# Ten short weight-merge chains placed elsewhere in a hand-written TensorE order (two attention blocks, one core)

## The chip, the cores and the metric

The kernel runs on one core of one Trainium2 chip. Its engines work side by side, each with its own instruction queue, in order: TensorE (PE, matmuls into PSUM), VectorE (DVE), ScalarE (ACT), GpSimd (POOL) and SyncE (SP), whose queue issues most DMAs. The metric is the device time of one launch in microseconds (us); lower is better. The time before is 253.73 us, the median of 3 runs (253.66 to 253.92).

## The reference, cut to what matters

Two independent attention blocks, A and B, each on an input of 2048 tokens x 640, with 32 heads of 20. A is softmax attention in a sliding window of 256 keys; B is linear attention. The two results are set side by side.

```python
def _A_ref(x, wqkv, wo):
    H = 32; Dh = D // H; W = 256
    qkv = (x @ wqkv).reshape(B, S, 3, H, Dh)              # -> q, k, v by head
    scores = einsum("bhqd,bhkd->bhqk", q, k) * Dh ** -0.5  # masked to 0 <= i - j < W
    p = softmax(scores)
    o = einsum("bhqk,bhkd->bhqd", p, v)
    return o.reshape(B, S, D) @ wo

def _B_ref(x, wqkv, wo):
    phi = lambda t: where(t > 0, t + 1, exp(t)) + 1e-6
    pq, pk = phi(q), phi(k)
    kv = einsum("bhsd,bhse->bhde", pk, v)
    z = einsum("bhsd->bhd", pk)
    num = einsum("bhqd,bhde->bhqe", pq, kv)
    den = einsum("bhqd,bhd->bhq", pq, z) + 1e-6
    return (num / den).reshape(B, S, D) @ wo

concatenate([_A_ref(...), _B_ref(...)], axis=-1)
```

All inputs are bfloat16.

## The kernel before

Tokens are worked in four blocks of 512 (`SB`), s = 0 to 3. The 640 input columns are five tiles of 128 (`KT`).

The frame of the program is A's attention. A list of units (`tiles_of`) fills a PSUM tile `S_ps` of four banks with scores (L789), ACT takes one exponential over all of it (L797), GpSimd clears the masked corners (`affine_select`, L812), and two units later `values` multiplies by v (L836). There is one `S_ps`, so the next unit's scores wait for the exponential. DVE turns the values (L849), divides by the row sums (L860, L866) into `N`, and DMA transposes (L877) make the layout `oT` for A's output product.

Between the units runs everything else, in the order of a hand-written `plan`: a list of entries with a due time (no unit, merely a place in the order). `at(t0, t1, gen, n)` spreads n steps of a generator evenly over t0 to t1. `fill_of` sorts the entries, and after each unit `take` draws so many matmul columns from them that all of the work is used up by the end. One step is in general one PSUM bank: a chain of five matmuls and its copy to SBUF. A chain may be cut by the next unit. The bank comes from a pool of four (`dps`, tile name `dense`), shared with the values; a chain can only start when the bank's last user has been read.

Who empties a bank is settled while the program is written. `evac` gives a plain copy to ACT (L259) or DVE (L261), by two counters of the work that each was given. `phi` (B's keys and queries) needs both: an exponential on ACT (L284), then two operations on DVE (L288, L291), the second of which reads the bank again. DMA issues that hang on these are put off by some banks with `soon` and then go to SP's queue in that order.

B's second half is what the change touches. `b_kv` builds the key-value product by head into `kv_T`; two selects on GpSimd (L623) keep each head's own block. `b_merge` then multiplies `kv_T` by B's output weights: ten banks (five tiles of 128 rows, two halves of 320 columns), each of two matmuls (L675) and a copy into the place of B's key weights in `wB`. `b_out` (B's output, through L274) reads these merged weights.

B's queries: `b_q(s)` makes five chains (L274, xB and wB), each with its `phi` and a DMA transpose of the result to tokens (L706, `tok`). `b_den` makes the denominators (L718, L729, L730). `quotients` multiplies the tokens by the reciprocals on DVE, four operations (L754), and turns each back with a DMA transpose (L758). `again_x` (L953) loads a block of x again from DRAM scratch. `a_out(s)` is A's output product of a block, five banks; `a_v(3)` A's last value projection (L409).

In plan times, the neighbourhood of the merges (46.0 to 52.8 before) is: `b_q(1)` 45 to 50, `a_v(3)` 43 to 49, `a_out(0)` (A's first output) 44.5 to 48.5, `b_den(0)` at 46.3, `a_out(1)` (A's second output) 50.2 to 54.8, `b_q(2)` 52 to 57, `b_den(1)` at 53, `b_out(0)` 54.8 to 59.2.

Of the kernel before, what the change touches and what calls it, by code (L numbers as in the profile page):

```python
# [92 lines left out]
def kernel(  # L93
# [12 lines left out]
    KT = D // P  # L106
# [146 lines left out]
    def evac(dst, src, n=SB, to=None):  # L253

        if to is None:
            to = "A" if load["A"] < load["D"] + AHEAD else "D"
        load[to] += n + COPY
        if to == "A":
            nc.scalar.activation(out=dst, in_=src, func=ACT.Copy)  # L259
        else:  # L260
            nc.vector.tensor_copy(out=dst, in_=src)  # L261

    def bank(wide=False):
        flush(begun[0] - 2)
        begun[0] += 1
        settle(False)
        if wide:
            return dps.tile([P, 2 * SB], BF16, name="dense")
        return dps.tile([P, SB], F32, name="dense")
# [396 lines left out]
    def b_merge():  # L666

        for c in range(KT):
            for lo in (0, D // 2):
                cols = slice(lo, lo + D // 2)  # L670
                ps = bank()
                for i in range(2):

                    at = PAD + (P - GD) * c - i * GD
                    nc.tensor.matmul(  # L675
                        ps[:, 0 : D // 2],
                        lhsT=kv_T[0:GD, c + i, at : at + P],
                        rhs=wo_sb["B"][0 : GH * DH, c + i, cols],
                        start=(i == 0),
                        stop=(i == 1),  # L680
                    )
                evac(w_sb["B"][:, c, D + lo : D + lo + D // 2], ps[:, 0 : D // 2], D // 2)
                yield End(D)
# [60 lines left out]
    def quotients(s):  # L744


        def one(tb):
            settle()
            add_load(d=1400)
            if tb == 0:  # L750
                oT_B[s] = xp.tile([P, KT, SB], BF16, name="xA")
            v = tok_of[s][:, tb, 0:D]
            vh = v.rearrange("p (h e) -> p h e", e=DH)
            nc.vector.tensor_tensor(  # L754
                out=vh, in0=vh, in1=rden_of[s][:, tb, :, :].to_broadcast([P, H, DH]), op=ALU.mult
            )
            out = oT_B[s][:, :, tb * P : (tb + 1) * P]
            soon(lambda: nc.sync.dma_start_transpose(out=out, in_=v), 1)  # L758

        quotients_due.extend((s, tb, one) for tb in range(TPS))  # L760
# [272 lines left out]
    plan = []  # L1033

    def at(t0, t1, gen, n):
        for i in range(n):
            plan.append((t0 + (i + 0.5) / n * (t1 - t0), gen, i == n - 1))

    def do(t0, t1, fns):
        fns = list(fns)  # L1040
        for i, fn in enumerate(fns):
            plan.append((t0 + (i + 0.5) / len(fns) * (t1 - t0), None, fn))
# [30 lines left out]
    for s, tq, td, tx in ((0, (39.5, 45), 46.3, 47.7), (1, (45, 50), 53, 54.3),  # L1073
# [1 line left out]
        at(*tq, b_q(s), KT)  # L1075
        at(td, td + 0.1, b_den(s), 1)
        do(tx, tx, [lambda s=s: quotients(s)])
    at(46.0, 52.8, b_merge(), 2 * KT)
    for n, s, t0, t1 in (("A", 0, 44.5, 48.5), ("A", 1, 50.2, 54.8), ("B", 0, 54.8, 59.2),
                         ("B", 1, 60.2, 64), ("A", 2, 64.4, 68.2), ("B", 2, 69, 73),  # L1080
                         ("B", 3, 73, 76)):
# [40 lines left out]
    for i, (s, parts, selects, done) in enumerate(units):  # L1122
# [7 lines left out]
        if ready and ready[0][0] + LAG <= i:  # L1130
# [3 lines left out]
            _, at = ready.popleft()  # L1134
# [10 lines left out]
    while ready:  # L1145
        take(5500)
        _, at = ready.popleft()
# [36 lines left out]
```

## Time and profile before

| | |
|---|---|
| time, median of 3 runs | 253.73 us (253.66 to 253.92) |
| profiled execution, time | 253.77 us |
| profiled execution, span | 252.1 us |
| granted TensorE clock | 0.998 |
| PE busy | 247.5 us (98%), 3733 matmuls |
| ACT busy | 196.6 us (78%) |
| POOL busy | 186.3 us (74%) |
| DVE busy | 167.4 us (66%) |
| merges (L675) in the trace | 20 matmuls, 162.1 to 184.1 us |

The span is what the profiler saw from the first to the last instruction; the time of the launch has 1.67 us more. The page's busy time of an engine says how long it had an instruction in work. In a row of the timeline come the start, the length, the engine, the line, the operation, the output and inputs with their shape and the number of instructions put together; a bracket gives the idle time ahead of the row and what ended it. Rows of PE overlap a little, as matmuls are pipelined: the distance from start to start is the better measure there. A row of the waits names who waited, for whom, the total, how often, and the longest.

### The profile page before, as it was taken

What the parts mean: (1) busy time and instruction counts of PE and PEld (TensorE: products, weight loads), DVE (VectorE), ACT (ScalarE), POOL (GpSimd) and SP (SyncE); (2) the same over time, 40 slices, a digit from 0 to 9 for tenths busy, and PEclk for the clock granted to TensorE, in tenths of its full rate; (3) what the DMA queues carried; (4) which work ended last, traced back from release to release, by engine and by line L of the source; (5) the groups of instructions that cost most, each with busy time, mean ns of one, the idle gap of its engine ahead of it and who ended that gap; (6) DMA issues with size and microseconds to landing.
All of it is one profiled execution on the core that took longest, in us unless ns stands there. A gap on an engine that the chain in (4) does not pass through costs nothing.

```text
span 252.1 us, 8786 instructions
## 1 busy us (share of the span) xinstructions
PE 247.5 (98%) x3733; PEld 142.4 (56%) x3733; DVE 167.4 (66%) x310; ACT 196.6 (78%) x194; POOL 186.3 (74%) x310
## 2 busy tenths in 40 slices
PE   8999999999999999999999999999999999999994
PEld 7644446557755446457445555556455565655573
DVE  0345777768644566776664766666879688869662
ACT  3376779898867788997658887889998998999541
POOL 1126798879877798686778969888887978999800
PEclk9999999999999999999999999999999999999999
DMA  6996598899650252997759595621957398869614
GB/s 204 321 264 160 107 194 130 157 213 245 91 104 3 70 167 34 235 248 186 80 124 165 107 202 99 168 26 38 194 109 157 83 194 173 114 161 146 196 56 155
DMA packets 68412, 37.04 MB, mean 147 GB/s; under 512 B 51605, under 2 KB 67349, under 8 KB 68373
## 3 DMA queue, kind: packets, MB, share of 16 engines
q1 hardware_dynamic: 67685, 35.67, 68.5%
q10 hardware_dynamic: 688, 0.82, 1.0%
q8 instruction: 29, 0.48, 0.8%
q14 instruction: 10, 0.08, 0.1%
HBM read 14.42 MB, written 9.83 MB: 96 GB/s over the span
## 4 chain that ended last, share of the span: by engine, by line
PE 93%; DVE 2%; ACT 2%; issue 1%; ACTq 0%
PE dense L274 52%; PE S_ps L789 11%; PE dense L564 9%; PE dense L836 9%; PE dense L409 7%; PE dense L196 1%; PE first L409 1%; PE dense L718 1%; PE first L178 1%; PE dense L675 1%; PE dense L647 1%; DVE phi L291 1%; DVE e L288 0%; ACT e L284 0%; PE dense L903 0%
## 5 line engine op out<-in xcount | busy, mean ns | idle before, releaser
L812 POOL TENSOR_SCALAR_AFFINE_SELECT p<-p 128x256 bf16<-128x256 bf16 (+2 forms) x280 | 176.5, 660 | 41.9 <-ACT p L797 40.4
L797 ACT ACTIVATE p<-S_ps 128x2048 bf16<-128x2048 f32 x76 | 142.8, 1879 | 33.8 <-PE S_ps L789 31.5
L274 PE MATMUL dense<-xA,wqk 128*128 128x512 bf16 x200 | 50.9, 380 | 0.1
L789 PEld LDWEIGHTS <-kpad 20*128 20x128 bf16 (+1 forms) x1216 | 21.7, 98 | 29.6 <-issue 26.0
L789 PE MATMUL S_ps<-qpad,kpad 20*65 20x64 bf16 (+3 forms) x1216 | 33.7, 228 | 0.0
L288 DVE TENSOR_SCALAR e<-e 128x512 bf16<-128x512 bf16 x40 | 18.6, 465 | 21.4 <-ACT e L284 21.2
L849 DVE STREAM_TRANSPOSE T<-dense 128x512 f32<-128x512 f32 x32 | 22.8, 712 | 15.0 <-PE dense L836 14.8
L274 PEld LDWEIGHTS <-wqk 128*128 128x128 bf16 x200 | 17.9, 98 | 19.5 <-POOL wqk L353 0.4
L291 DVE SCALAR_TENSOR_TENSOR phi<-dense,e 128x512 bf16<-128x512 f32 x40 | 27.7, 692 | 1.6
L274 PE MATMUL dense<-xB,wB 128*128 128x512 bf16 x100 | 26.3, 380 | 0.0
L836 PE MATMUL dense<-p,vA 128*32 128x64 bf16 (+2 forms) x1216 | 25.9, 231 | 0.0
L274 PE MATMUL dense<-wB,xB 128*128 128x512 bf16 (+1 forms) x160 | 25.9, 300 | 0.0
L564 PE MATMUL dense<-tok,phi 128*128 128x129 bf16 (+1 forms) x160 | 25.5, 300 | 0.0
L274 PE MATMUL dense<-wo,oT 128*128 128x512 bf16 (+4 forms) x165 | 25.1, 296 | 0.0
L284 ACT ACTIVATE e<-dense 128x512 bf16<-128x512 f32 x40 | 23.6, 597 | 1.2 <-PE dense L274 1.0
L274 PE MATMUL dense<-wB,xA 128*128 128x512 bf16 (+1 forms) x160 | 24.3, 299 | 0.0
L409 PE MATMUL dense<-wA,xA 128*128 128x320 bf16 x140 | 24.0, 301 | 0.1
L836 PEld LDWEIGHTS <-vA 128*32 128x32 bf16 x1216 | 19.4, 97 | 3.8 <-issue 0.8
L259 ACT ACTIVATE osb<-dense 128x512 bf16<-128x512 f32 (+2 forms) x28 | 15.8, 580 | 5.3 <-PE dense L274 5.2
L409 PEld LDWEIGHTS <-xA 128*128 128x128 bf16 x160 | 15.0, 98 | 7.8 <-ACT xA L347 0.5
L754 DVE TENSOR_TENSOR tok<-tok,rden 128x640 bf16<-128x640 bf16 x16 | 17.8, 1115 | 0.3 <-DMA tok<-phi 0.3
L866 DVE TENSOR_TENSOR N<-T,recA 128x320 bf16<-128x320 f32 (+1 forms) x28 | 15.5, 553 | 3.3 <-DMA oT<-N 2.4
(65 smaller groups left out, 197.5 us busy)
## 6 DMA issues: line engine op xcount, KB each, us to landing
out_dram<-osb SPq DMA_DIRECT2D x7, 640.0 KB
x_scr<-xB SPq DMA_DIRECT2D x4, 640.0 KB
tok<-in_B_x_dram SPq DMA_DIRECT2D x4, 640.0 KB
xB<-x_scr SPq DMA_DIRECT2D x4, 640.0 KB
wB<-in_B_wqkv_dram SPq DMA_DIRECT2D x3, 800.0 KB
q_scr<-qpad SPq DMA_DIRECT2D x16, 60.0 KB
k_scr<-kpad SPq DMA_DIRECT2D x16, 60.0 KB
qpad<-q_scr SPq DMA_DIRECT2D x16, 60.0 KB
```

Of the source, the lines that this page charges most:

```text
L274: nc.tensor.matmul(dst, lhsT=lhs(kt), rhs=rhs(kt), start=(kt == 0), stop=(kt == KT - 1))
L284: nc.scalar.activation(out=view(e), in_=src, func=ACT.Exp)
L288: nc.vector.tensor_scalar(out=e[:], in0=e[:], scalar1=1e-6, scalar2=1.0 + 1e-6, op0=ALU.add, op1=ALU.min)
L291: nc.vector.scalar_tensor_tensor(out=dst, in0=src, scalar=0.0, in1=view(e), op0=ALU.max, op1=ALU.add)
L409: nc.tensor.matmul(ps[:, 0 : hh * DH], lhsT=xt[:, kt, tb * P : (tb + 1) * P], rhs=w_sb["A"][:, kt, i * hh * DH : (i + 1) * hh * DH], start ...
L564: nc.tensor.matmul(out, lhsT=pk[:, tb, c * P : (c + 1) * P], rhs=x[:, tb, lo:hi], start=(i == 0), stop=(i == len(blocks) - 1),)
L754: nc.vector.tensor_tensor(out=vh, in0=vh, in1=rden_of[s][:, tb, :, :].to_broadcast([P, H, DH]), op=ALU.mult)
L789: nc.tensor.matmul(S_ps[0:keys, j, col : col + n], lhsT=k_pad[kb // TPS][rows, g, ko : ko + keys], rhs=q_pad[s][rows, g, q0 : q0 + n], sta ...
L797: nc.scalar.activation(out=p, in_=S_ps[:], func=ACT.Exp, scale=scale)
L812: nc.gpsimd.affine_select(out=dst, in_=v, pattern=[[0, 4], [0, n], [sgn, w]], compare_op=ALU.is_ge, fill=0.0, base=base, channel_multiplie ...
L836: nc.tensor.matmul(O_ps[32 * j : 32 * (j + 1), q0 : q0 + n], lhsT=v_flat[kb // TPS % 3][:, at + j * HV : at + j * HV + 32], rhs=p[:, j, co ...
L849: nc.vector.transpose(out=T.rearrange("p b e -> p (b e)"), in_=O_ps[:])
```

## The change

The ten banks of `b_merge` are no longer spread evenly from 46.0 to 52.8. They get ten places written out. Before, they stood at 46.34, 47.02, 47.70, 48.38, 49.06, 49.74, 50.42, 51.10, 51.78 and 52.46. Now eight lie before 50.2, where A's second output begins, and the last two between its chains. What the merges compute, and everything else in the plan, is left as it was. Since the pool of banks, the choice of the copying engine and the put-off DMA issues follow from the order, these change for the neighbouring chains too.

```diff
-    at(46.0, 52.8, b_merge(), 2 * KT)
+
+    merges = b_merge()
+    for i, t in enumerate((46.1, 46.5, 46.9, 47.4, 47.9, 48.4, 48.9, 49.3, 51.1, 52.4)):
+        plan.append((t, merges, i == 2 * KT - 1))
```

## The prediction

> **What bounds the kernel now.** I read the page's busy times first, then the list of what TensorE (PE) waited for, then the timeline of PE, ScalarE (ACT), VectorE (DVE) and the DMA issues (SPq) around the change, 160 to 200 us. From the page, from the waits of PE, and from the timeline of PE:
>
> ```profile
> PE 247.5 (98%) x3733; PEld 142.4 (56%) x3733; DVE 167.4 (66%) x310; ACT 196.6 (78%) x194; POOL 186.3 (74%) x310
> ...
> PE dense L675 <- DVE phi L291: 0.3, 1, 0.3
> ...
> 166.66 0.46 PE L789 MATMUL S_ps<-qpad,kpad 20*128 20x320 bf16 x20
> 167.15 0.85 PE L836 MATMUL dense<-p,vA 128*32 128x256 bf16 x40
> ...
> 179.35 1.24 PE L274 MATMUL dense<-wo,oT 128*128 128x512 bf16 x5
> 180.94 0.43 PE L675 MATMUL dense<-wo,kv_T 120*128 120x320 bf16 x2 [0.34 <-DVE phi L291]
> 181.31 0.59 PE L274 MATMUL dense<-wo,oT 128*128 128x512 bf16 x2
> ...
> 198.48 0.81 PE L274 MATMUL dense<-xB,wB 128*128 128x512 bf16 x3
> ```
>
> PE is busy 98% and, between its start and its last matmul, waits once: before the eighth merge, whose PSUM bank still holds a query chain of B that DVE's phi reads. Start to start shows the price better than the 0.34: chains of five 128x512 matmuls follow each other after 1.08 (193.94 to 195.02), so 180.43 was due and 180.94 came (0.51); the merge pair itself then took 0.37 instead of the 0.28 of the pair at 176.99 (0.09 to get going again). A second, smaller loss has no bracket: the score group at 166.66 took 0.49 to the values behind it, others take 0.39; the values' bank was still being copied by ACT (wB at 166.66 for 0.44). Together 0.70 us. More than that the change cannot win in this stretch; PE's work is the same, in another order.
>
> The end of the span hangs on PE, so only what makes PE wait counts. What can make it wait are four PSUM banks that rotate. ACT empties some, in order, behind softmax exponentials of 1.88; DVE others:
>
> ```profile
> 176.14 1.88 ACT L797 ACTIVATE p<-S_ps 128x2048 bf16<-128x2048 f32 x1 [0.25 <-PE S_ps L789]
> 177.91 0.43 ACT L259 ACTIVATE vA<-dense 128x320 bf16<-128x320 f32 x1
> 178.55 0.61 ACT L284 ACTIVATE e<-dense 128x512 bf16<-128x512 f32 x1
> 179.04 1.89 ACT L797 ACTIVATE p<-S_ps 128x2048 bf16<-128x2048 f32 x1
> ...
> 192.49 0.78 DVE L754 TENSOR_TENSOR tok<-tok,rden 128x640 bf16<-128x640 bf16 x1
> 196.31 0.36 DVE L288 TENSOR_SCALAR e<-e 128x512 bf16<-128x512 bf16 x1 [1.37 <-ACT e L284]
> 196.71 0.69 DVE L291 SCALAR_TENSOR_TENSOR phi<-dense,e 128x512 bf16<-128x512 f32 x1
> ...
> 190.92 0.53 SPq L953 DMA_DIRECT2D xB<-x_scr  x1
> 191.88 1.22 SPq L758 DMA_TRANSPOSE xA<-tok  x1
> 196.53 2.50 SPq L706 DMA_TRANSPOSE tok<-phi  x2
> ...
> SPq L706 <- DMA xA<-tok: 3.3, 1, 3.3
> ```
>
> The reader should see that ACT has no gap between 176.14 and 179.04, that DVE has one of 1.37 before 196.31, and that a transposing DMA issued at 191.88 was only done by 196.5: the next one waited 3.3 us for it.
>
> **The change, part by part.** Nothing is added or removed. A merge is two matmuls (0.28) and one copy (0.32 from start to next start on ACT, 0.37 on DVE), with no DMA. The built program gives the order and the bank of each chain. The first merge stays at 162.06, so its inputs (the selects on kv_T that end at 160.8, the load of wo) cost what they did. Merges 2 to 8 move ahead of chains of the value projection, of A's first output and of B's queries for block 1; 9 and 10 go between A's second output's chains.
>
> What goes. The small wait at 167.15 goes: that bank is now merge 2's, copied by DVE some 1.5 us earlier (-0.10). The one at 180.94 goes: the merge in that place, behind the first chain of A's second output, is now the ninth, and its bank was last used by the eighth (-0.60).
>
> What is late next. Merges 7 and 8 now come right behind a value-projection chain, and the last query chain (c = 4) follows them in the bank of that chain, copied by ACT. Up to the score group before it, PE has lost the 0.10 wait and 0.10 of work has moved behind it: the group of 175.54 starts at 175.34 and ends 0.39 later, 175.73. ACT's exponential starts 0.21 after (175.93 to 176.14) at 175.94; the next instruction 1.77 later (176.14 to 177.91), 177.71; that is the exp of query chain 3, 0.49 (178.55 to 179.04); then the value copy from 178.20, done at 178.63. PE goes from 175.73 through values 0.78, one matmul 0.21, the value chain 0.68 and two merges 0.56 to 177.96, and can start at 178.68 (0.05 after the release, as from phi's end 180.89 to 180.94). Lost: 0.72, and 0.09 to get going: **0.81**. Three chains on, the values wait in the same way for ACT's copy of the first chain of A's second output: PE there at 182.3, copy done at 182.45, **0.2**. Net of both sides: 1.0 - 0.7 = **+0.3**. Bounds: nothing at all lost at the second place and ACT 0.2 sooner gives -0.1; ACT's two copies swapped late by 0.3 gives +0.6. I take +0.3; it follows from durations that hardly vary on ACT (1.88, 0.44, 0.60).
>
> **The moved DMA.** Query chain 4 also carries a DMA: its phi is turned to tokens by a transpose on SP's queue. Before, the transposes of chains 3 and 4 were issued at 177.50 and 183.33. Now chain 3's takes the second of these places and chain 4's is queued behind three of A's output transposes, one of B's divided tokens and the reload of x (190.92): the place of the transpose at 191.88. DVE's first product of the tokens with the reciprocal (192.49, L754) waits for all five transposes of its block. DVE is in order: behind the product stand a reciprocal, the normalisation, another product and then e and phi of the next query chain, whose bank PE wants at 198.48.
> Issue: 191.88, or up to 0.9 sooner, as the 1.5 us of the transpose at 177.50 no longer hold back the one at 179.11, which is then bound by its product of 177.70, moved to 177.3 (done 178.1). I take 191.0. Landing: no row shows this transfer, so from its neighbours: 4.6 from issue at this very place (191.88 to 196.5), 3.5 for the one issued at 219.93 (its product started at 223.43), 4.6 for an oT transpose of 132.4 that a normalisation waited for until 137.01. I take 4.6, the same place behind the same reload: done at **195.6**; ends 194.5 and 196.5.
> DVE arrives at 192.49 + 0.3 = 192.8 and waits 2.8. From 192.49 to phi's end at 197.40 it needed 4.91, of them 1.37 idle: 3.54 of work. So phi ends at 195.6 + 3.5 = 199.1 and PE, due at 198.48 + 0.3 = 198.8, starts at 199.15: 0.35 + 0.09 = **+0.45**. Ends: landing at 194.5 gives 198.0, nothing; 196.5 gives 200.05, 1.25 + 0.09 = 1.35. The banks wanted after that (200.06 and 201.1) are free by then, and DVE's next gap (1.36 before 202.22) takes up the rest.
>
> A rule bears on this landing. The Trainium skill, "DMA: Bandwidth & Descriptors", section "Anatomy of one DMA", fits, for DMAs on the GpSimd path, a fixed 2.0 us plus bytes over 436 GB/s. For these 131 KB that is an estimate of 2.3 us, a landing before 194, and a sum of +0.3 alone. The row above, at the same place of the queue, says 4.6, so I let the row decide.
>
> Nothing else: GpSimd's order is unchanged, and over the rest of the program one copy moves from ACT to DVE near the end, where DVE idles 0.3 to 0.9 before each of its copies after 232 us: nothing, at worst 0.2. The last merge ends at 184.2 as before, and B's first output reads the merged weights from 193.94.
>
> **Sum.** The profiled execution took 253.77 for a span of 252.1 (1.67 around it), 0.04 above the median of the runs. 252.1 + 0.3 + 0.45 + 1.67 = 254.52; against the median 253.73 + 0.75 = **254.5**.
>
> **Rivals.**
> 1. Only the banks: the tokens land by about 195.2, or DVE makes up the time. Speaks for it: the landing of 3.5, and the gap of 1.37 on DVE. Against: the row at 191.88. 253.73 + 0.3 = 254.0, within 0.2%. The fit of the Trainium skill above would give this one.
> 2. Faster: the waits of 0.70 go and chain 4 finds its bank free. It decides at the value copy: it would have to end before 178.0, 0.6 sooner than worked out. ACT would have to start the exponential ahead of it at 175.3, before its scores end at 175.73, or to take the copy out of turn; that speaks against it. For it: ACT's start and PE's end are each read from one row. With no new wait 253.0, with the 0.2 behind it 253.2.
> 3. The late tokens cost in full: landing at 196.5 or later, and the products at their slow durations (1.06 and more). +0.3 + 1.35 = 255.4.
>
> **How the numbers follow.** About 0.2% (0.51 us; 253.22 and 254.24) is what a measurement here can tell from no change. Forecast (banks and a token wait that PE feels, 254.1 to 255.0): 0.50, of it 0.06 still within 0.2%. Rival 1: 0.30, nearly all within, 0.02 above. Rival 2: 0.09, of it 0.07 faster by enough. Rival 3: 0.11. So slower 0.57, same 0.36, faster 0.07. The range for 8 in 10 leaves out rival 2 and the far part of rival 3: 253.7 to 255.4. The likeliest one's own is 254.1 to 255.0.
>
> **What would show it.** Right: no wait of L675 for phi at 180.9; PE instead idles some 0.7 near 178 before a chain of xB and wB, for ACT's copy of vA; a DVE wait of 2 to 3.5 us of L754 for the DMA of tok from phi near 193; a PE wait near 199 for phi L291. Wrong: no DVE wait near 193, or one that PE does not feel (rival 1); no gap near 178 (rival 2); PE waits that are spread over the region after 200 us, which I have not worked out.

## The result, and the profile after

The changed kernel takes **255.38 us** (median of 6 runs, 255.09 to 256.27) beside 253.93 us for the kernel before on the same chip (6 runs, 253.66 to 254.42): a ratio of 1.0054, 95% interval 1.0035 to 1.0072. It is 1.45 us slower, where 0.75 was forecast; the time lies at the very end of the range (253.7 to 255.4).

The profiled execution is the slowest of the six: 256.27 us for a span of 254.5 (the other five have spans of 253.4 to 254.0). It shows each cost, but one of them larger than in the median run; which one comes out below.

The busy times of the page of after, then the rows of PE's list of waits that matter:

```profile
PE 247.3 (97%) x3733; PEld 142.2 (56%) x3733; DVE 166.9 (66%) x311; ACT 196.3 (77%) x193; POOL 185.9 (73%) x310
...
PE dense L274 <- DVE phi L291: 1.5, 1, 1.5
...
PE dense L274 <- ACT vA L259: 0.6, 1, 0.6
PE dense L836 <- DVE osb L261: 0.5, 1, 0.5
```

PE's work is the same 247 us. The one wait of before (a merge for phi) is gone, and three new ones stand there. (A fourth, 0.4 for the load of wA, belongs to the first ten microseconds, of which more below.) In the timeline of PE after (start, length, line; the bracket is the idle time ahead of the row) they are here:

```profile
177.51 0.71 PE L675 MATMUL dense<-wo,kv_T 120*128 120x320 bf16 x4
178.78 0.38 PE L274 MATMUL dense<-xB,wB 128*128 128x512 bf16 x1 [0.56 <-ACT vA L259]
...
197.88 1.04 PE L274 MATMUL dense<-wB,xA 128*128 128x512 bf16 x4
200.43 0.81 PE L274 MATMUL dense<-xB,wB 128*128 128x512 bf16 x3 [1.51 <-DVE phi L291]
...
238.20 3.20 PE L274 MATMUL dense<-wB,xA 128*128 128x512 bf16 x14
241.90 0.85 PE L836 MATMUL dense<-p,vA 128*32 128x256 bf16 x40 [0.49 <-DVE osb L261]
```

Two merges take 1.27 from start to start instead of 0.56; four matmuls at 197.88 take 2.55 instead of 0.88; fourteen at 238.20 take 3.70 where the same row in before took 3.13. Rows of before for the last two (the next row there starts at 198.48):

```profile
197.60 1.04 PE L274 MATMUL dense<-wB,xA 128*128 128x512 bf16 x4
...
236.28 3.20 PE L274 MATMUL dense<-wB,xA 128*128 128x512 bf16 x14
239.41 0.85 PE L836 MATMUL dense<-p,vA 128*32 128x256 bf16 x40
```

Behind the second wait stand these rows of SP's queue and of DVE, after:

```profile
190.29 0.51 SPq L953 DMA_DIRECT2D xB<-x_scr  x1
190.91 1.21 SPq L706 DMA_TRANSPOSE tok<-phi  x1
...
192.14 0.70 DVE L849 STREAM_TRANSPOSE T<-dense 128x512 f32<-128x512 f32 x1
196.48 0.82 DVE L754 TENSOR_TENSOR tok<-tok,rden 128x640 bf16<-128x640 bf16 x1 [3.63 <-DMA tok<-phi]
...
199.69 0.69 DVE L291 SCALAR_TENSOR_TENSOR phi<-dense,e 128x512 bf16<-128x512 f32 x1
```

The transpose of the last query chain's tokens is issued at 190.91 right behind the reload of x, and DVE, done with its row of 192.14 at 192.8, waits 3.63 us for it; phi, two products later, ends at 200.38, and PE goes on at 200.43. Behind the third wait, from DVE after:

```profile
239.08 0.25 DVE L860 RECIPROCAL recA<-T 128x16 f32<-128x16 f32 x1
239.37 0.70 DVE L866 TENSOR_TENSOR N<-T,recA 128x128 bf16<-128x128 f32 x1
240.00 1.25 DVE L866 TENSOR_TENSOR Nr<-T,recA 128x192 bf16<-128x192 f32 x1
241.16 1.27 DVE L261 CAST osb<-dense 128x512 bf16<-128x512 f32 x2
```

and from ACT before, where the first of those copies was ACT's and in time:

```profile
237.19 0.60 ACT L259 ACTIVATE osb<-dense 128x512 bf16<-128x512 f32 x1 [0.76 <-PE dense L274]
```

**A table by stages.** Runs of one kernel differ by a microsecond or more, part of it from the first ten microseconds, where PE waits 0 to 1.9 us for the load of wA (L409). To compare kernels I therefore cut every profile at the same five points of PE's order: the scores groups of 16 matmuls (L789, 20x256) that start at 140.51, 169.66, 184.74 and 199.22 in before, the first row of 128x128 matmuls after 234 (L274, 234.35), and the end of PE's last row (248.85). Between two points lies the same work in all kernels, up to the places of the merges. The entries are differences of start times, in us; the last column is the sum of the five less before's.

| kernel | 140 to 170 | to 185 (banks) | to 199 (tokens) | to 234 | to the end (tail) | against before |
|---|---|---|---|---|---|---|
| before | 29.15 | 15.08 | 14.48 | 35.13 | 14.50 | |
| after | 28.89 | 15.55 | 16.15 | 35.10 | 15.06 | +2.41 |
| after, second profile | 28.90 | 15.55 | 16.54 | 35.10 | 15.06 | +2.81 |
| late_product | 28.90 | 15.54 | 14.48 | 35.39 | 15.06 | +1.03 |
| late_reload | 28.90 | 15.54 | 14.48 | 35.10 | 15.06 | +0.74 |
| tail_before | 28.89 | 15.55 | 14.77 | 35.09 | 14.49 | +0.45 |
| before_late_tokens | 29.15 | 15.08 | 16.11 | 35.09 | 14.50 | +1.59 |
| late_reload_and_tail | 28.90 | 15.54 | 14.48 | 35.13 | 14.49 | +0.20 |
| before_tail_swapped | 29.16 | 15.08 | 14.48 | 35.11 | 15.05 | +0.54 |
| late_product_and_tail | 28.89 | 15.55 | 14.48 | 36.42 | 14.50 | +1.50 |
| before_late_reload | 29.15 | 15.08 | 14.48 | 35.12 | 14.50 | -0.01 |
| other_times | 29.06 | 14.78 | 14.48 | 35.14 | 14.50 | -0.38 |
| other_times_early_reload | 29.05 | 14.79 | 16.10 | 35.09 | 14.50 | +1.59 |

The stages repeat within some hundredths wherever the order and the copies' engines are the same, except the token stage. So the change has three separate terms: banks -0.26 + 0.47 = **+0.21**, tokens **+0.3 to +2.1** by the run, tail **+0.56**.

### The profile page after: what moved, and what is told of

It reads as the page before. It is cut to its first block, busy times and chain, and to the rows that moved or that the text cites. A ratio compares the mean times of both kernels' runs of the same rounds, so it can differ in the third digit from the quotient of the medians.

```text
span 254.5 us, 8787 instructions
## 1 busy us (share of the span) xinstructions
PE 247.3 (97%) x3733; PEld 142.2 (56%) x3733; DVE 166.9 (66%) x311; ACT 196.3 (77%) x193; POOL 185.9 (73%) x310
## 4 chain that ended last, share of the span: by engine, by line
PE 88%; DMA 4%; DVE 3%; issue 2%; ACT 2%; SPq 0%; ACTq 0%
PE dense L274 49%; PE S_ps L789 11%; PE dense L564 9%; PE dense L836 8%; PE dense L409 7%; DMA wA<-in_A_wqkv_dram 2%; DMA xA<-tok 2%; PE first L409 1%; PE dense L675 1%; PE dense L718 1%; ACT e L284 1%; PE dense L647 1%; DVE phi L291 1%; DVE Nr L866 0%; DVE e L288 0%
## 5 line engine op out<-in xcount | busy, mean ns | idle before, releaser
L274 PE MATMUL dense<-xA,wqk 128*128 128x512 bf16 x200 | 50.9, 380 | 0.1
L789 PEld LDWEIGHTS <-kpad 20*128 20x128 bf16 (+1 forms) x1216 | 21.7, 98 | 30.4 <-issue 27.0
L789 PE MATMUL S_ps<-qpad,kpad 20*65 20x64 bf16 (+3 forms) x1216 | 33.7, 227 | 0.0
L288 DVE TENSOR_SCALAR e<-e 128x512 bf16<-128x512 bf16 x40 | 19.4, 486 | 21.3 <-ACT e L284 21.2
L274 PEld LDWEIGHTS <-wqk 128*128 128x128 bf16 x200 | 17.9, 98 | 19.5 <-issue 0.4
L274 PE MATMUL dense<-xB,wB 128*128 128x512 bf16 x100 | 26.6, 380 | 2.1 <-DVE phi L291 1.5
L274 PE MATMUL dense<-wB,xB 128*128 128x512 bf16 (+1 forms) x160 | 25.9, 300 | 0.0
L274 PE MATMUL dense<-wo,oT 128*128 128x512 bf16 (+4 forms) x165 | 25.1, 296 | 0.0
L284 ACT ACTIVATE e<-dense 128x512 bf16<-128x512 f32 x40 | 23.6, 598 | 1.2 <-PE dense L274 1.0
L274 PE MATMUL dense<-wB,xA 128*128 128x512 bf16 (+1 forms) x160 | 24.3, 299 | 0.0
L409 PE MATMUL dense<-wA,xA 128*128 128x320 bf16 x140 | 23.5, 299 | 0.5 <-DMA wA<-in_A_wqkv_dram 0.4
L259 ACT ACTIVATE osb<-dense 128x512 bf16<-128x512 f32 (+2 forms) x29 | 16.5, 581 | 6.5 <-PE dense L274 6.4
L409 PEld LDWEIGHTS <-xA 128*128 128x128 bf16 x160 | 15.0, 98 | 8.4 <-issue 0.5
L754 DVE TENSOR_TENSOR tok<-tok,rden 128x640 bf16<-128x640 bf16 x16 | 15.9, 991 | 3.8 <-DMA tok<-phi 3.6
```

Of the source, the lines that this page charges most:

```text
L274: nc.tensor.matmul(dst, lhsT=lhs(kt), rhs=rhs(kt), start=(kt == 0), stop=(kt == KT - 1))
L284: nc.scalar.activation(out=view(e), in_=src, func=ACT.Exp)
L288: nc.vector.tensor_scalar(out=e[:], in0=e[:], scalar1=1e-6, scalar2=1.0 + 1e-6, op0=ALU.add, op1=ALU.min)
L409: nc.tensor.matmul(ps[:, 0 : hh * DH], lhsT=xt[:, kt, tb * P : (tb + 1) * P], rhs=w_sb["A"][:, kt, i * hh * DH : (i + 1) * hh * DH], start ...
L789: nc.tensor.matmul(S_ps[0:keys, j, col : col + n], lhsT=k_pad[kb // TPS][rows, g, ko : ko + keys], rhs=q_pad[s][rows, g, q0 : q0 + n], sta ...
```

## The experiments

My theory after the result: the three terms are independent, and the middle one comes from one DMA that lands late. The rivals: the new rotation of the banks makes PE late everywhere and the DMA is only beside it; or the DMA is late by its place in the queue alone, not by what is transferred beside it. In the kernels named here as having their copies' engines written out, the choice between ACT and DVE is read from the list that after (or before) made of its 136 copies, so that an edit cannot shift it:

```diff
-
-        if to is None:
-            to = "A" if load["A"] < load["D"] + AHEAD else "D"
+        if picks:
+            to = picks.pop(0)
```

### late_product: DVE comes later to the tokens

```diff
-    for s, tq, td, tx in ((0, (39.5, 45), 46.3, 47.7), (1, (45, 50), 53, 54.3),
+    for s, tq, td, tx in ((0, (39.5, 45), 46.3, 47.7), (1, (45, 50), 53, 55.4),
```

> The kernel after, with the engine of every copy written out as it is there, and one entry of the plan changed: the products with the quotient (L754) of B's second segment stand 1.1 later in the plan, behind other work of DVE. Theory (the tokens of the fifth query chain land late, and DVE's in-order product waits for them, and PE for the phi behind it): DVE waits under 0.5 us for the tokens, PE's wait of 1.5 us near 200 us is gone, and the time falls by what that wait costs in the median run, 0.4 to 0.9 us, to 254.5 to 255.0. Rival (the new rotation of banks itself makes PE late, the tokens only happen to be late beside it): a PE wait of over 1 us stays near 200 us, and the time stays at 255.4. Second rival (the wait is passed on to what needs the product, the transposes of L758 and B's second output): the wait near 200 us goes and another of about 1 us comes behind it, 255.2 to 255.6.

Measured: 255.93 us (255.41 to 256.33) beside 254.22 for before, ratio 1.0069 (1.0050 to 1.0087). The mechanism is as the theory has it: DVE waits no longer for the tokens, PE's wait is gone, the token stage is 14.48 as in before. The time did not fall, so the theory's number failed. In the profile 0.26 went on to the stage from 199 to 234 us, as the second rival has it: ten matmuls at 209.93 take 2.46 from start to start (2.17 in before), and the row behind them starts as a phi behind the later products ends (212.34). That is too little for the time: by its stages the profile is 1.03 over before, the median is 1.71 over. No run here tells what the other 0.7 is.

### late_reload: the transpose ahead of the reload of x

```diff
-    for s, t0, t1 in ((0, 2, 33.5), (1, 12, 38.5), (2, 26.2, 45.5), (3, 30.2, 51.2)):
+    for s, t0, t1 in ((0, 2, 33.5), (1, 12, 38.5), (2, 26.2, 45.5), (3, 30.2, 53.2)):
```

> The kernel after, copies' engines written out, and the reload of x for B's last segment (L953) put later in the plan, so that it stands behind the late token transpose in SP's queue and not ahead of it. If the transpose is late because of its place in the queue alone: it is issued 0.5 us sooner, lands 5.5 us after that, DVE waits 3.1 us instead of 3.6 and PE about 1.0 instead of 1.5: 254.9. If it is late because the reload's transfer lies beside it: it lands under 4.5 us after its issue, DVE waits under 2.2 us and PE under 0.2: 254.5 to 254.8. If the tokens are not the cause: 255.4 with the PE wait as it was.

Measured: 255.21 us (254.09 to 255.85) beside 254.22, ratio 1.0035 (1.0021 to 1.0050). SP's queue and DVE in this kernel:

```profile
190.63 1.19 SPq L706 DMA_TRANSPOSE tok<-phi  x1
191.92 1.22 SPq L758 DMA_TRANSPOSE xA<-tok  x1
193.57 0.35 SPq L953 DMA_DIRECT2D xB<-x_scr  x1
...
192.79 0.71 DVE L849 STREAM_TRANSPOSE T<-dense 128x512 f32<-128x512 f32 x1
193.42 0.79 DVE L754 TENSOR_TENSOR tok<-tok,rden 128x640 bf16<-128x640 bf16 x1
```

The product starts as soon as DVE is free: the tokens were there 2.8 us after their issue, or sooner. In after they took 5.5 (190.91 to 196.45, less the 0.03 at the start of the product). The issue itself came 0.93 sooner against PE (190.63 - 185.67 = 4.96 behind the scores group of the table, 5.89 in after); that alone would have left 2.7 of DVE's 3.63. The rest is the landing, sooner after the issue by 2.7 or more. What moved in the DMA engines from 0.6 to 2.6 us after the transpose's issue, first in after (191.5 to 193.5), then here (191.2 to 193.2):

```profile
DMA packets 93, 0.48 MB, mean 238 GB/s; under 512 B 0, under 2 KB 0, under 8 KB 93
...
DMA packets 715, 0.17 MB, mean 83 GB/s; under 512 B 715, under 2 KB 715, under 8 KB 715
```

In after it is the reload alone (93 packets of some 5 KB), in late_reload only small packets, those of the transposes. So it is the reload's 640 KB ahead of the transpose that makes it late, not its place among the issues alone. The 254.5 to 254.8 expected of that case were 0.57 to 0.87 over the before of the first chip; against the before of this one, which is 0.29 higher, the stages give +0.74, as expected, and the medians +0.99, 0.1 more than expected.

### tail_before: the copies of the tail on the engines of before

Four of the copies from B's first output on go to another engine in after than in before: the fourth of B's first output, the last of A's third, the fourth of B's third and the first of B's last. They are the 106th, 117th, 121st and 123rd of the 136 (D for DVE, A for ACT), and are set back here, in the list that late_product has.

```diff
-    picks = list("ADAADADADADADDDDDDDDDADDDADDAADDADDADDDDAADADDDDADDADDDDADADDAADDDDADDDADDADDDDADADADDDDAADAAAAAAADADAAAAAAAAAAAAAAADDADADDADAADADADADAD")
+    picks = list("ADAADADADADADDDDDDDDDADDDADDAADDADDADDDDAADADDDDADDADDDDADADDAADDDDADDDADDADDDDADADADDDDAADAAAAAAADADAAAADAAAAAAAAAAADADDDAADAADADADADAD")
```

> The kernel after, with every copy's engine written out as there up to B's third segment, and from there on as in the kernel before, so that the first bank of B's last output is copied by ACT again and not by DVE behind the normalisation (L866). Theory (that copy is the third term, which the prediction put at nothing): PE's wait for DVE's osb near 242 us falls from 0.5 us to under 0.1, and the time by 0.4 to 0.6 us, to 254.8 to 255.0. Rival (there is slack behind it, the output's transfers or the copies that follow end last anyway): 255.3 to 255.5.

Measured: 255.04 us (254.27 to 256.19) beside 254.22, ratio 1.0045 (1.0028 to 1.0062). The timeline of PE here, to be held against 238.20 and 241.90 in after:

```profile
237.20 3.20 PE L274 MATMUL dense<-wB,xA 128*128 128x512 bf16 x13
240.33 0.85 PE L836 MATMUL dense<-p,vA 128*32 128x256 bf16 x40
```

3.13 from start to start and no wait; the tail stage is 14.49, as in before. (Thirteen matmuls instead of fourteen: a record is missing.) The expectation speaks of the copies from B's third segment on; the list also sets back the 106th, in B's first output. Here its engine is worth nothing: the stage that holds it, 199 to 234, is 35.09 beside 35.10 in after. This profile also shows how much the token term moves by itself, since nothing in that stage was edited:

```profile
189.91 1.20 SPq L706 DMA_TRANSPOSE tok<-phi  x1
...
195.08 0.82 DVE L754 TENSOR_TENSOR tok<-tok,rden 128x640 bf16<-128x640 bf16 x1 [1.85 <-DMA tok<-phi]
```

Issued 4.5 us after the scores group of the table (5.9 in after), landed 5.1 later, DVE waited 1.85 and PE lost 0.29.

### before_late_tokens: that DMA alone

```diff
-    oT_B = {}
+    oT_B, late = {}, []
...
-            phi(pq[:, c, :], ps[:], then=lambda fn=to_tokens: soon(fn, 2))
+            phi(pq[:, c, :], ps[:], then=lambda fn=to_tokens, q=(s, c): late.append(fn) if q == (1, KT - 1) else soon(fn, 2))
...
-    do(21.5, 21.5, [lambda: nc.gpsimd.memset(kv_T[:], 0.0)])
+    do(21.5, 21.5, [lambda: nc.gpsimd.memset(kv_T[:], 0.0)]); do(52.5, 52.5, [lambda: late.pop()()])
```

> The kernel before, with one part of the change alone: the token transpose of the fifth query chain of B's second segment is held back until after the reload of x, which is where the change puts it; merges, banks and copies stay as before. Theory: DVE waits 2.5 to 4 us for the tokens at its product, PE 0.5 to 1.7 us near 200 us, and the time rises by 0.4 to 1.6 us, to 254.3 to 255.5. Rival (the rotation of banks alone): no new PE wait over 0.2 us, 253.8 to 254.1.

Measured: 255.73 us (7 runs, 255.59 to 258.18) beside 254.22, ratio 1.0080 (1.0051 to 1.0110). Before's banks and tail, and one held-back transpose, cost as much as the whole change. From DVE and PE of this kernel:

```profile
196.41 0.92 DVE L754 TENSOR_TENSOR tok<-tok,rden 128x640 bf16<-128x640 bf16 x1 [3.48 <-DMA tok<-phi]
...
200.46 0.81 PE L274 MATMUL dense<-xB,wB 128*128 128x512 bf16 x3 [1.47 <-DVE phi L291]
```

The same two rows as in after (3.63 and 1.51), without any moved merge. The rival that the rotation of the banks is what makes PE late near 200 us is out.

### after_again, late_reload_and_tail, other_times, before_tail_swapped

These four ran on one chip beside a before of 254.18 us (29 runs). after_again is the changed kernel once more, with no edit.

> The kernel after, unchanged, on the chip of the three that follow. What the earlier profiles lead to: PE stands 0.2 to 0.3 us later than in before once the banks are through, its wait near 242 us for DVE's osb is 0.5 us again, and the wait near 200 us for the phi behind the late tokens takes any value from 0.2 to 1.5 us, by when SP issues and the transfer lands: 254.9 to 255.6 beside a before of 253.9 to 254.3. Rival (the wait near 200 us is fixed): 1.4 to 1.7 us again.

Measured: 255.74 us (255.48 to 257.82), ratio 1.0074 (1.0048 to 1.0099); the median is above the 255.6 that was set as the end. The bank stage and the tail are the same to 0.01; the token wait is not:

```profile
201.98 0.81 PE L274 MATMUL dense<-xB,wB 128*128 128x512 bf16 x3 [1.91 <-DVE phi L291]
```

1.91 here, 1.51 in the first profile. Over the profiles of this token order PE lost 0.29, 1.67 and 2.06 us in that stage; the median of the runs, +1.45 and +1.56 over before, leaves 0.7 to 0.8 for it once the 0.21 and 0.56 are taken off. That last is worked out, not seen in a profile, and holds to some tenths only: late_reload, with no such loss in its profile, lies 0.99 over before in the median for 0.74 in the stages.

late_reload_and_tail is late_reload with the four copies of tail_before.

> The kernel after with two of its three costs taken out: the reload of x (L953) stands behind the late token transpose, and from B's third output on the copies go to the engines of before. Theory (bank step, late tokens and tail copy are all there is): PE has no wait over 0.2 us near 200 us and near 242 us, the loss that stays is the bank step's 0.2 to 0.3 us, and the time is 0.1 to 0.5 us over before's of the same chip. Rival (something else in the change costs): 0.7 us or more over before.

Measured: 254.37 us (254.05 to 255.47), ratio 1.0015 (1.0002 to 1.0029): 0.19 over before, and +0.20 by the stages. With the late transfer and the tail copy out, only the bank step is left; the change has no fourth cost.

other_times moves the reload as late_reload does, and the merges to other places; no engine is written out.

```diff
-    for i, t in enumerate((46.1, 46.5, 46.9, 47.4, 47.9, 48.4, 48.9, 49.3, 51.1, 52.4)):
+    for i, t in enumerate((46.5, 47.4, 47.4, 48.4, 48.4, 48.9, 49.3, 49.3, 51.6, 52.0)):
...
-    for s, t0, t1 in ((0, 2, 33.5), (1, 12, 38.5), (2, 26.2, 45.5), (3, 30.2, 51.2)):
+    for s, t0, t1 in ((0, 2, 33.5), (1, 12, 38.5), (2, 26.2, 45.5), (3, 30.2, 53.2)):
```

> As in late_reload_and_tail for the reload, with no engine written out, and other times for the merges (the first eight from 46.5 to 49.3, two of them twice at one time, the last two at 51.6 and 52.0), so that the bank of the last query chain is free sooner and the copies' engines in the tail come out as in before by themselves. Theory (the 0.7 us that before loses at its eighth merge are really won, and only what took their place hid it): PE's wait for ACT's vA near 178 us is under 0.3 us, none is over 0.2 us near 200 us and in the tail, and the time is 0.1 to 0.5 us under before's of the same chip. Rival (a wait as long appears elsewhere whenever the merges move): 0 to 0.5 us over before.

Measured: **253.77 us** (253.03 to 254.06) beside 254.18, ratio 0.9982 (0.9973 to 0.9991): faster than both kernels. The place that cost PE 0.7 in after, in the timeline of PE:

```profile
177.54 1.00 PE L675 MATMUL dense<-wo,kv_T 120*128 120x320 bf16 x6
178.67 0.38 PE L274 MATMUL dense<-xB,wB 128*128 128x512 bf16 x1
```

Six matmuls that take 0.84 (0.28 a pair) take 1.13: the loss is 0.3 instead of 0.7. Three merges instead of two stand ahead of the last query chain, but that is not what saves it, since other matmuls moved ahead of the scores group in turn: PE gets there 2.57 behind the group that starts at 175.81, and got there 2.64 behind the same group (175.43) in after. What differs is the order on ACT, first in after, then here:

```profile
176.03 1.88 ACT L797 ACTIVATE p<-S_ps 128x2048 bf16<-128x2048 f32 x1 [0.49 <-PE S_ps L789]
177.80 0.59 ACT L284 ACTIVATE e<-dense 128x512 bf16<-128x512 f32 x1
178.28 0.45 ACT L259 ACTIVATE vA<-dense 128x320 bf16<-128x320 f32 x1
...
175.78 0.60 ACT L284 ACTIVATE e<-dense 128x512 bf16<-128x512 f32 x1
176.41 1.88 ACT L797 ACTIVATE p<-S_ps 128x2048 bf16<-128x2048 f32 x1
178.18 0.43 ACT L259 ACTIVATE vA<-dense 128x320 bf16<-128x320 f32 x1
```

The exponential of the query chain before (L284) no longer stands between the softmax exponential and the copy of vA, so the copy is done 2.80 behind the scores group instead of 3.30. The two bank stages together are 0.39 shorter than before's. What the change set out from is real; it needs the wait that takes its place to be short, too.

before_tail_swapped is the kernel before with the four tail copies on the engines that after gives them.

> The kernel before with one consequence of the change alone: from B's third output on, the copies go to the engines that they have in after, written out; merges, banks and transfers stay. Theory (the first bank of B's last output, copied by DVE behind L866, is a term by itself): PE's wait for DVE's osb near 240 us comes up with 0.4 to 0.6 us, and the time is 0.4 to 0.6 us over before's. Rival (it costs only because the tokens or the banks had already put DVE late): no wait over 0.1 us, and within 0.2 us of before.

Measured: 254.71 us (254.07 to 255.69), ratio 1.0018 (1.0005 to 1.0031), 0.53 over before. The wait came up in before as well, with the size that it has in after:

```profile
240.41 0.85 PE L836 MATMUL dense<-p,vA 128*32 128x256 bf16 x40 [0.49 <-DVE osb L261]
```

So the tail copy is a term by itself, and DVE's lateness from the tokens has no part in it. (Here too the edit takes in the 106th copy, which the expectation leaves out; its stage is 35.11 beside 35.13 in before.)

### late_product_and_tail, before_late_reload, other_times_early_reload

These ran beside a before of 254.30 us (29 runs).

> late_product with the tail's copies on the engines of before as well. By the stages of the profiles (PE's distance from one scores group to the next) the bank step costs 0.21 us, the tail nothing, and the product that stands later 0.26 to 0.29 us between 200 and 235 us; the start, where PE waited 1.9 us for wA in the profile of late_product and 0 to 1.0 in the others, has nothing to do with the edit. Theory: DVE does not wait for the tokens, PE's stage from 185 to 200 us is as long as in before (14.5 us), and the time is 0.3 to 0.7 us over before's of the same chip. Rival (what late_product's time showed over its stages, about 0.7 us, belongs to the later product): 1.0 us or more over before, by stages after 200 us that are longer.

Measured: 255.78 us (255.27 to 256.17), ratio 1.0048 (1.0029 to 1.0068), 1.48 over before. The rival's time came, and so did its longer stage: 199 to 234 us is 1.29 longer than before's, where late_product had 0.26. Its reason is not borne out, as the rows show. PE here:

```profile
207.26 0.85 PE L836 MATMUL dense<-p,vA 128*32 128x320 bf16 x40 [0.59 <-DVE osb L261]
...
212.70 0.59 PE L274 MATMUL dense<-wB,xA 128*128 128x512 bf16 x2 [0.51 <-DVE phi L291]
```

and DVE:

```profile
201.85 1.28 DVE L754 TENSOR_TENSOR tok<-tok,rden 128x640 bf16<-128x640 bf16 x1
203.24 0.99 DVE L288 TENSOR_SCALAR e<-e 128x512 bf16<-128x512 bf16 x1
204.27 0.69 DVE L291 SCALAR_TENSOR_TENSOR phi<-dense,e 128x512 bf16<-128x512 f32 x1
204.88 1.73 DVE L754 TENSOR_TENSOR tok<-tok,rden 128x640 bf16<-128x640 bf16 x1
206.53 0.68 DVE L261 CAST osb<-dense 128x512 bf16<-128x512 f32 x1
```

The four products, put later to spare DVE the wait, now run between 200 and 208 without a gap among phi and copies that PE's banks hang on. What this kernel has over late_product comes from its edit: the 106th copy, one of the four that are set back, lies in this stage. late_product makes it on ACT, and its DVE goes from the third product to the fourth at once:

```profile
205.60 2.71 DVE L754 TENSOR_TENSOR tok<-tok,rden 128x640 bf16<-128x640 bf16 x2
...
206.18 0.59 ACT L259 ACTIVATE osb<-dense 128x512 bf16<-128x512 f32 x1
```

The third product starts 4.63 behind the scores group of the table in both (200.97 there, 200.25 here), so up to this point the two do not differ. Then the copy stands between the products here; it is done 6.96 behind the group instead of 5.80, PE waits 0.59 for it, and the ten matmuls ahead of the later wait for phi take 2.84 from start to start instead of 2.46. With the products at their earlier place the engine of this copy was worth nothing (35.09 beside 35.10, 35.11 beside 35.13). The wait was passed on, as the second rival of late_product has it, by 0.26 there; the rest of the 1.29 is the copy's. What late_product's median has over its stages stays open.

> The kernel before with the reload of x (L953) moved as in late_reload, and nothing else. Theory (in before the tokens land before DVE wants them, so where the reload stands is worth nothing, and the gain of other_times is the merges' own): no stage differs from before by over 0.1 us, and the time is within 0.2 us of before's. Rival (the reload is worth something by itself): 0.3 to 0.5 us faster.

Measured: 254.21 us (253.94 to 254.53), ratio 0.9984 (0.9961 to 1.0008), every stage within 0.01 of before. The reload's place is worth nothing in before; the 0.39 that other_times wins in the stages is the merges'.

> other_times with the reload where before has it, ahead of the late token transpose. Theory: the merges win 0.4 us as in other_times, and the token transpose lands beside the reload's transfer again, 4.5 to 6 us after its issue; DVE waits 1.5 to 3.5 us for it and PE 0 to 1.3 us near 200 us, so that the time lies 0.3 us under to 0.9 us over before's, and over that of other_times. Rival (the transfer's neighbour does not matter, the place of the merges does): as other_times, 0.3 to 0.5 us under before.

Measured: 254.86 us (254.04 to 255.74), ratio 1.0019 (0.9997 to 1.0040). The interval takes in no change; against before it says little, but the median is 0.56 above its own before where that of other_times was 0.41 below, some 1.0 apart, and the profile says why. The bank stages are those of other_times; the token stage is 16.10, with

```profile
190.26 0.51 SPq L953 DMA_DIRECT2D xB<-x_scr  x1
190.88 1.22 SPq L706 DMA_TRANSPOSE tok<-phi  x1
...
196.28 1.08 DVE L754 TENSOR_TENSOR tok<-tok,rden 128x640 bf16<-128x640 bf16 x1 [3.33 <-DMA tok<-phi]
```

The transpose right behind the reload lands 5.4 us after its issue, for other merges and other banks.

## Why the prediction was right or wrong

The forecast was slower by 0.75 us through the banks and a token wait; measured is slower by 1.45. The sign and both places were right. The sum was not: one term (the landing of the tokens) was too small, and one (the copies further on) was put at nothing.

1. *What goes.* Right. No merge waits for phi at 180.9 any more.
2. *The new bank waits, +0.3 net.* Right: +0.21 in the stages, in all seven profiles with these merges (28.89 or 28.90, and 15.54 or 15.55). The wait for ACT's copy of vA, put at 0.72 with a start at 178.68, is 0.71 with a start at 178.78 (1.27 instead of 0.56). The values' wait, put at 0.2, is 0.18 (0.57 instead of 0.39 from the row at 181.99).
3. *The moved DMA, +0.45.* The place, the chain (transpose, product, normalisation, phi, PE) and the issue (forecast 191.0, measured 190.91) were right, the size was not. The term that failed is the landing: "I take 4.6, the same place behind the same reload". It was 5.1 to 5.5 us in the four profiles with this order where it can be read (both of after, tail_before, other_times_early_reload). The row it came from, a transpose issued at 191.88 in before, stood 0.96 behind the reload's issue; the moved one stands 0.62 to 0.91 behind it. Counted from the reload's issue the landing is 5.6 us in before, 5.9 to 6.2 in those four and 6.5 in before_late_tokens, where the transpose was issued 2.2 behind the reload: it hardly lands sooner for an earlier issue. In after none of its small packets moves from 191.5 to 193.5, while the reload's do; the reload's last go before 194.5, and the landing is 2.0 behind that. The time from the transpose's own issue should not have been carried over; the time from the reload's should. DVE then needed 3.9 from landing to phi's end, not 3.5 (its products and its e took 0.82, 1.06 and 0.76). Both together put PE's loss at 1.67 in this profile, above the upper end of 1.35. With 0.29 and 2.06 in the other two the term has no single value; the median runs carry some 0.7 to 0.8 of it.
4. *"Nothing else ... at worst 0.2".* Wrong. The copy that moves from ACT to DVE near the end costs 0.56. I counted DVE's idle time ahead of its copies after 232 us (0.3 to 0.9), but not that at this copy's due time DVE starts the reciprocal and the normalisation of the last values but one, 2.1 us in one piece; what mattered was the work ahead of it in DVE's order, not the idle share around it. Nor was it "one copy": from B's first output on four copies change their engine, two each way.
5. *The rivals.* Of the three, the third (late tokens in full, 255.4, chance 0.11) gave the measured time, but by another sum: 0.3 + 1.35 there, 0.21 + 0.56 + 0.7 in the median run. That the measured time still lies inside the range is in part luck: the tail's 0.56 was not in the sum, and the token loss ran from 0.29 to 2.06 between profiles of one order. Rival 1 fails (the wait is there and PE feels it), rival 2 too: ACT's exponential started at 176.03, not at 175.3.
6. *The rule that I weighed.* The fixed 2.0 us plus bytes over 436 GB/s that the Trainium skill fits for DMAs on the GpSimd path ("DMA: Bandwidth & Descriptors", "Anatomy of one DMA") made an estimate of 2.3 us for this transpose, which SP issues. With the reload issued behind it, it lands in at most 2.6 us (other_times, issued 190.09, product at 192.70) to 2.8, which does not contradict that estimate; with the reload ahead it takes 5.1 to 5.5. To let the row decide was right for the order that the change makes; the rule would have told what an order without the reload ahead is worth.

What stays open: why SP issues this transpose 4.5 us after the scores group in one profile (tail_before) and 5.6 to 6.3 in others with the same order of issues. The rows that differ are its issues before it (the first L877 took 1.41 and the L758 1.24 in tail_before, 2.33 and 1.99 in after); what they waited for the profiles do not tell.

## What to carry to other kernels

When a chain is moved, follow its DMA: look which large transfer is issued ahead of it on the same queue, count the landing from that transfer's issue (5.6 to 6.5 us here), and move the large transfer behind the small one if nobody waits for it (with the merges of other_times one number in the plan, 53.2 for 51.2, was worth some 1.0 us, the merges 0.4). Where a program chooses engines by running counters, list every choice that a change flips and look at what stands ahead of each in its new engine's order; the idle share of the engine does not price it. A wait for a rotating buffer is not removed by moving its user: find what the buffer waits for in the new order, and what stands ahead of that copy on its engine.

## What was not expected

- A 131 KB transpose took at most 2.6 to 2.8 us from issue to landing with the 640 KB reload issued behind it, and 5.1 to 5.5 with the reload issued 0.6 to 0.9 us ahead of it.
- In three profiles with the same order (tail_before, after, after_again) SP's issue of one and the same transpose row (L758) took 1.24, 1.99 and 2.36 us, and PE lost 0.29, 1.67 and 2.06 us in the token stage, while every other stage that was not edited repeated within 0.01.
- PE's wait for the first load of wA, before 10 us, was 0 to 1.9 us over profiles whose program is the same up to there, and moved everything behind it: the first point of the table lies at 140.51 to 142.05.
